# The last group of heads but one in the last segment: products with V in column tiles, brought back through DRAM

## The chip, the cores and the metric

The kernel runs on one core of a Trainium2 chip (the chip has eight). The metric is the time of one execution on the device in microseconds (us); the time of a kernel is the median over its runs. The engines of a core run side by side, each through its own instructions in order: TensorE (PE, matmuls; PEld is its loading of weights), VectorE (DVE), ScalarE (ACT), GpSimd (POOL) and SyncE (SP), which here only issues DMAs. Results of PE land in PSUM, everything else lies in SBUF or in DRAM.

## The reference

The input x (2048 tokens of 640) is normalized. One branch is an attention with a memory, over four segments of 512 tokens and 32 heads of 20 columns; the other is a gated unit; their product, after an output projection and a silu, is added to x:

```
for s in range(N):                       # N = 4 segments of L = 512
    logits = einsum('bhqd,bhkd->bhqk', qs, ks) * scale + mask
    p = softmax(logits, axis=-1)
    a_dot = einsum('bhqk,bhkd->bhqd', p, vs)
    a_mem = einsum('bhld,bhde->bhle', pq, M) / (einsum('bhld,bhd->bhl', pq, z) + 1e-6)
    o = g * a_mem + (1.0 - g) * a_dot
    M, z = M + pk^T vs, z + sum(pk)
...
h = sigmoid(xn @ w_gate) * (xn @ w_up)
return x + (o @ wo) * silu(h @ w_down)
```

The mask is causal within a segment, phi is applied to q and k for the memory.

## The kernel before, in words

Heads come in eight groups of four (20 columns each, so a group is 80 columns of the 640). A segment has 20 slots, five for a pair of groups; the whole kernel has 80 slots and an empty one behind them, number 80. In a slot PE computes scores for one unit of the lower triangle (`scores`, into `Sps`), ScalarE takes the exponential (`exps`, into `pt`, of which there are four), and GpSimd zeroes what lies above the diagonal. Four buffers of PSUM (tag "d") go round among all other products.

The products with V are made in one of two ways.

- In column tiles (`attend_T`, L556): V is the stationary operand, one head for each quarter of the array's columns, and `ApsT` comes out transposed, 16 matmuls for a group. Then VectorE turns it in blocks of 32 (`turn`, into `tb`), the quotients are taken (`quotients`: a reciprocal on VectorE and two multiplications, on GpSimd but for group 7, where they are on VectorE; into `ob`) and VectorE turns it back (`turn_back`, into `obT`). `dot_spill` (four DMAs on SP's queue, one for each head of a group) writes that to DRAM (`OTd`), where the columns lie in the order of the output projection; `out_load` reads it back as `oT`, five chunks of 128 columns, and `out_add` adds the memory's part (`oTm`), which came through DRAM by a transposing DMA.
- Naturally (`attend`, L593): `pt` is the stationary operand, V moves, 40 matmuls of 21 columns for a group into `Aps`; `finalize` (four VectorE operations: rd, rd, od, odot) divides and adds the result to the memory's part in `odot`, tokens on partitions.

All groups go the first way, but for groups 6 and 7 of the last segment, whose slots begin at `OLD` = 75. There `attend` runs behind slots 75 to 79. Their columns are 480 to 640, that is a quarter of chunk 3 (from `C3` = 384) and chunk 4 (from `C4` = 512). Chunk 3 comes back by a spill of `odot` and a transposing DMA (`tail_spill`, `tail_T`), to which `tail_sum` adds the 96 columns that came the first way; chunk 4 is transposed by PE (`tail_T4`, two transposes each for the first and the second half of the tokens, into `po`) and copied to `oT` by ScalarE.

Between the slots' own work a planner lays out the dense matmuls: `gp` and `up` (the gated unit), `yp` (its down projection, 12 matmuls each, followed by a tanh `t` on ScalarE and a product `aa` on VectorE), the projections, and events, each with a due time in slots from the table `TIMES` and a cost in ns. The dense work is spread evenly. In the slot ahead of each `attend_T` (a visit) the dense matmuls are issued in column tiles as well (`ORDER["columns"]`, in the profile "128*32", four for one). The last two down projections are held back: behind all slots come the first of them, `tail_T4(0, 2)`, and the output projection of the first 128 tokens (`tail_piece`, two products `sp` of five matmuls, each multiplied into `aa` by VectorE; `tail_add` adds x and issues the store), then the second of them, and the other pieces, with `tail_T4(2, 4)` among them.

The order on each engine is that of the program's text: nothing is reordered behind it.

Of the kernel before, what the change touches and what calls it, by code (L numbers as in the profile page):

```python
# [50 lines left out]
def segment_units(n):  # L51
# [3 lines left out]
    return units  # L55

TIMES = dict(
    turn=(0.03, 0.27, 1.29), turn_last=(0.0, 0.135, 0.43), attend=0.36, rest=350, dot6=0.43, load6=0.48,
    dot7=1.92, load7=1.95, add=(4.27, 4.52), out=(5.25, 5.95, 7.25, 8.35, 8.74, 9.06, 9.45, 11.05), update=-1.2,
    mem=(2.23, 4.32, 3.0, 6.98, 6.98, 2.45, 9.09, 10.79), mem_spill=11.56, mem_T=14.4, mem_T_last=12.63,  # L60
    k_tok=2.04, dot3=13.22, dot5=17.84, load5=18.1, add5=19.86, stats0=(0.53, 0.9, 1.65, 3.6),
    stats=(-0.55, 0.13, 1.32, 3.57), norm=(5.26, 5.72, 6.03, 6.29), norm_T=7.22, ready=12.0,
    K=(9.69, 10.07, 10.49, 13.82, 14.29), Q=(11.32, 11.72, 12.29, 12.45, 13.52), K_eng='vaava', Q_eng='avvav',
    V=(10.33, 13.33, 14.43, 14.63, 17.05, 17.66, 19.78, 20.06), V_eng='avaavvav', k_spill0=14.77, k_lay0=15.15,
# [5 lines left out]
def mm_ns(n):  # L70
    return n / 2.4 + 3.0
# [4 lines left out]
def kernel(  # L76
# [420 lines left out]
            out_store(n, j)  # L497

    C3, C4 = (DC - 2) * P, (DC - 1) * P
    CUT = 6 * 4 * DH - C3  # L500
    tail = {}

    def tail_spill():
        nc.sync.dma_start(Od[(NSEG - 1) % 2][:, C3:C4].rearrange("(j p) d -> p j d", p=P),
                          seg[NSEG - 1]["odot"][:, :, C3:C4])

    def tail_T():
        nc.sync.dma_start_transpose(out=seg[NSEG - 1]["oTm"][:, 3, :], in_=Od[(NSEG - 1) % 2][:, C3:C4])

    def tail_sum():  # L510
        oTm = seg[NSEG - 1]["oTm"][0:CUT, 3, :]
        nc.vector.tensor_tensor(oTm, oTm, seg[NSEG - 1]["oT"][0:CUT, 3, :], op=ALU.add)

    def tail_T4(j0, j1):
        po = ps_d.tile([P, 2, P], BF, name="po", tag="d")
        for j in range(j0, j1):
            nc.tensor.transpose(po[:, j - j0, :], seg[NSEG - 1]["odot"][:, j, C4:D], ident[:])
        nc.scalar.copy(seg[NSEG - 1]["oT"][:, DC - 1, j0 * P:j1 * P].rearrange("p (j t) -> p j t", t=P), po[:])

    def tail_piece(j, half):  # L520

        s, hs = seg[NSEG - 1], slice(half * HD, (half + 1) * HD)
        sp = ps_d.tile([P, HD], F32, name="sp", tag="d")
        for c in range(DC):
            oT = s["oTm" if c == 3 else "oT"]
            nc.tensor.matmul(sp[:], lhsT=oT[:, c, j * P:(j + 1) * P], rhs=Wo[:, c, hs],  # L526
                             start=(c == 0), stop=(c == DC - 1), skip_group_check=True)
        nc.vector.tensor_tensor(s["aa"][j][:, hs], s["aa"][j][:, hs], sp[:], op=ALU.mult)

# [26 lines left out]
    def attend_T(n, g, todo):  # L556


        s = seg[n]
        if g % 4 == 0:  # L560
            s["obT", g // 4] = opool.tile([P, 4, L], BF, name="obT", bufs=1)
        ps = ps_d.tile([P, L], F32, name="ApsT", tag="d")
        for i, ((_, kb, c0, ncol, q0), t) in enumerate(todo):
            for r in range(4):
                off = (kb * H + 4 * g + r) * E1
                nc.tensor.matmul(ps[32 * r:32 * r + 32, q0:L], lhsT=Vflat[n % 2][:, off:off + 32],  # L566
                                 rhs=t[:, r, c0:c0 + ncol], start=(i == 0), stop=(i == len(todo) - 1),
                                 tile_position=(0, 32 * r), skip_group_check=True)
        tb = opool.tile([P, L // 32, 32], F32, name="tb", tag="tb", bufs=1)
        rb = opool.tile([P, L // 32], F32, name="rb", bufs=2)  # L570
        ob = obs[g % 2]

        def turn():
            nc.vector.transpose(tb[:].rearrange("p h e -> p (h e)"), ps[:].rearrange("p (a t b) -> p a b t", t=32, b=2))  # L574

        def quotients():
            nc.vector.reciprocal(rb[:], tb[:, :, DH])
            to = ob[:].rearrange("p a e b -> p a b e")[:, :, :, 0:DH]
            of = tb[:].rearrange("p (a b) e -> p a b e", b=2)[:, :, :, 0:DH]
            by = rb[:].rearrange("p (a b) -> p a b", b=2).unsqueeze(3).to_broadcast([P, L // 64, 2, DH])  # L580
            eng = nc.vector if g == NG - 1 else nc.gpsimd
            eng.tensor_scalar(rb[:], rb[:], omgT[:, g:g + 1], None, op0=ALU.mult)
            eng.tensor_tensor(to, of, by, op=ALU.mult)  # L583

        def turn_back():
            nc.vector.transpose(s["obT", g // 4][:, g % 4, :].bitcast(F32),  # L586
                                ob[:].rearrange("p a e b -> p (a e b)").bitcast(F32))

        s["turn", g] = (turn, quotients, turn_back)

    acc = dict(group=None, todo=[])

    def attend(n, unit, pt):  # L593

        todo = acc["todo"] + [(p, pt) for p in unit]
        acc["todo"] = []
        for i, ((g, kb, c0, ncol, q0), t) in enumerate(todo):
            if acc["group"] is None:
                acc["group"], acc["blocks"], acc["fresh"] = g, 0, True
                acc["ps"] = ps_d.tile([P, 4, 4, E1], F32, name="Aps", tag="d")  # L600
            if acc["group"] != g or (acc["blocks"] == 0 and i > 0 and todo[i - 1][0][0] != g):
                acc["todo"] = todo[i:]
                break
            for r in range(4):
                for qb in range(kb, 4):
                    off = c0 + (qb - kb) * P
                    nc.tensor.matmul(acc["ps"][:, qb, r, :], lhsT=t[:, r, off:off + P],
                                     rhs=V[n % 2][:, kb, 4 * g + r, :],
                                     start=acc["fresh"], stop=True, skip_group_check=True)
                    acc["fresh"] = False  # L610
            acc["blocks"] += 1
            if acc["blocks"] == 4:
                finalize(n, g, 0, 4)
                acc["group"] = None
                acc["todo"] = todo[i + 1:]
                break

    def finalize(n, g, q0, q1):

        s, Aps = seg[n], acc["ps"]  # L620
        nq = q1 - q0
        rd = opool.tile([P, 4, 4], F32, name="rd", bufs=3)
        nc.vector.reciprocal(rd[:, 0:nq, :], Aps[:, q0:q1, :, DH])
        nc.vector.tensor_tensor(rd[:, 0:nq, :], rd[:, 0:nq, :],
                                omg[:, 4 * g:4 * g + 4].unsqueeze(1).to_broadcast([P, nq, 4]), op=ALU.mult)
        dst = s["odot"][:, q0:q1, 4 * g * DH:(4 * g + 4) * DH]
        od = opool.tile([P, 4, 4 * DH], BF, name="od", tag="tb", bufs=1)[:, 0:nq, :]
        nc.vector.tensor_tensor(od.rearrange("p q (r e) -> p q r e", e=DH), Aps[:, q0:q1, :, 0:DH],
                                rd[:, 0:nq, :].unsqueeze(3).to_broadcast([P, nq, 4, DH]), op=ALU.mult)
        nc.vector.tensor_tensor(dst, dst, od, op=ALU.add)  # L630
# [102 lines left out]
        finish(do_up(0, f))  # L733

    GLU_NS, V_NS, AV_NS = DC * mm_ns(L), DC * mm_ns(HD), 700
    MEM_NS, C_NS = 220, 2 * mm_ns(L) + 200
    dense = deque()
    downs, outs = [0] * NSEG, [0] * NSEG
# [22 lines left out]
    def at(t, ns, fn, *a):  # L761
        events.append((t, len(events), ns, lambda: fn(*a)))

    visits = {}
    for p in range(0, OLD, 5):
        n, g = units[p][0], units[p][1][0][0]
        visits[p + 4] = (n, g, (p, p + 1, p + 2))
        visits[p + 6] = (n, g + 1, (p + 3, p + 2, p + 4))

    def out_item(n, i):  # L770
        while downs[n] < 8:
# [6 lines left out]

    for slot, (n, g, _) in visits.items():
        for k in range(3):  # L780
            at(slot + TIMES["turn_last" if g == NG - 1 else "turn"][k], 0, turn, n, g, k)

    def old_attend(slot):
        attend(NSEG - 1, units[slot][1], pts[slot])

    for slot in range(OLD, SLOTS - 1):
        at(slot + 1 + TIMES["attend"], 500, old_attend, slot)

    st = {}

# [11 lines left out]
    for n in range(NSEG):  # L802
# [22 lines left out]
        if n == NSEG - 1:  # L825
            on("dot5", 0, dot_spill, (n, 4, 6))
            on("load5", 0, out_load, (n, 0, 6 * 4 * DH))
            on("add5", 0, out_add, (n, 0, 3))
            continue
        m = n + 1  # L830
        on("stats0" if n == 0 else "stats", 0, stats, *[(m, j) for j in range(4)])
# [23 lines left out]
                    at(t0 + t, 0, fn, *a)  # L855
        if n + 2 < NSEG:
            on("load_x", 0, load_x, (n + 2,))
    at(SLOTS - 2.001, 0, tail_spill)
    at(SLOTS - 1.001, 0, tail_T)
    at(SLOTS - 0.001, 0, tail_sum)  # L860

    events.sort(key=lambda e: e[:2])
    events = deque(events)
# [32 lines left out]
    for slot, (n, unit) in enumerate(units):  # L896
# [24 lines left out]
        if cur[0] is not None and cur[0][0] * cur[0][1] < TIMES["rest"]:  # L921
            complete()
    fill(1e12)
    finish(held[1][3])
    tail_T4(0, 2)
    tail_piece(0, 0)
    tail_piece(0, 1)
    tail_add(0, 0, 2, nc.gpsimd, nc.sync)
    finish(held[0][3])
    tail_piece(1, 0)  # L930
    tail_piece(1, 1)
    tail_add(1, 0, 1, nc.vector)
    tail_T4(2, 4)
    tail_piece(2, 0)
    tail_add(2, 0, 1, nc.gpsimd, nc.scalar)
    tail_add(1, 1, 2, nc.vector)
# [35 lines left out]
```

## Time and profile before

| | us |
|---|---|
| median of three runs | 318.75 (318.68, 318.75, 319.62) |
| the profiled execution, its own time | 319.31 |
| its span, first to last instruction | 317.6 |
| PE busy | 308.5 (97%) |
| ScalarE busy | 226.9 (71%) |
| VectorE busy | 223.7 (70%) |
| GpSimd busy | 133.7 (42%) |
| moved by DMA | 41.36 MB |

All times in the traces are from the start of the span, and the span is 1.7 us shorter than the execution's own time. A row of a timeline gives start, length, engine, line, operation, what it writes and reads, and how many were merged; in brackets the engine's idle time before it and what ended that. A row of the chain of waits gives start, length and what held the end up in that stretch. A row of windows gives the stretch, its length, the busy time of PE, PEld, DVE, ACT and POOL with their instructions, the granted clock of PE as a share, the DMA engines' busy share and GB/s. PE's granted clock is full (1.00) over the whole span.

### The profile page before, as it was taken

To read this page: it belongs to the slowest core of one execution; us is meant where nothing else is said; L and a number is where in the kernel's file an instruction comes from. 1 tells how busy PE (TensorE), PEld (TensorE's weight loads), DVE (VectorE), ACT (ScalarE), POOL (GpSimd) and SP (SyncE) were. 2 spreads that over 40 slices of the span, in tenths; PEclk is the share of its full clock that TensorE was granted. 3 is DMA by queue.
4 is the path that set the end of the run, shared out by engine and by line. 5 is a ranking of instruction groups with operands and counts; after the bars stand their busy time and mean duration, and the time that the engine had idled before them with its cause. 6 is when DMAs were issued, how large, how long until landed. Compare 5 with 4: busy or idle time off the path is not lost.

```text
span 317.6 us, 10039 instructions
## 1 busy us (share of the span) xinstructions
PE 308.5 (97%) x4212; PEld 166.7 (52%) x4241; DVE 223.7 (70%) x504; ACT 226.9 (71%) x228; POOL 133.7 (42%) x230
## 2 busy tenths in 40 slices
PE   7999999999999999999999999999999999999995
PEld 3544445665545445654665455545466655445673
DVE  6474445655868988888769989788777686634465
ACT  3723477778798776777987869678896776777711
POOL 1870035435253445335444354454544353535412
PEclk9999999999999999999999999999999999999999
DMA  7984886510742362405943475139524001250312
GB/s 254 370 320 142 284 229 169 137 33 2 219 138 76 102 160 106 105 23 157 254 143 109 121 138 147 49 114 216 168 82 122 19 23 44 92 137 4 99 20 83
DMA packets 56085, 41.36 MB, mean 130 GB/s; under 512 B 26952, under 2 KB 54664, under 8 KB 56040
## 3 DMA queue, kind: packets, MB, share of 16 engines
q1 hardware_dynamic: 53496, 35.97, 40.3%
q10 hardware_dynamic: 2544, 4.75, 4.0%
q8 instruction: 33, 0.54, 0.7%
q14 instruction: 12, 0.10, 0.1%
HBM read 19.90 MB, written 14.78 MB: 109 GB/s over the span
## 4 chain that ended last, share of the span: by engine, by line
PE 94%; issue 1%; DMA 1%; ACT 1%; DVE 1%; SPq 0%; ACTq 0%
PE yp L124 11%; PE up L124 11%; PE gp L124 10%; PE psq L124 10%; PE Sps L542 9%; PE gp L128 6%; PE up L128 6%; PE yp L128 5%; PE ApsT L566 5%; PE psv L124 5%; PE psq L128 4%; PE sp L124 3%; PE sp L128 3%; PE psv L128 2%; PE sp L526 1%
## 5 line engine op out<-in xcount | busy, mean ns | idle before, releaser
L550 ACT ACTIVATE pt<-Sps 128x2048 bf16<-128x2048 f32 x80 | 150.3, 1879 | 41.5 <-PE Sps L542 39.8
L552 POOL TENSOR_SCALAR_AFFINE_SELECT pt<-pt 128x512 bf16<-128x512 bf16 x128 | 82.9, 663 | 157.2 <-ACT pt L550 154.7
L432 DVE SCALAR_TENSOR_TENSOR hT<-tg,up 128x512 bf16<-128x512 bf16 x48 | 32.6, 679 | 24.0 <-PE up L124 10.0
L124 PE MATMUL up<-xnT,Wu 128*128 128x512 bf16 x146 | 40.3, 380 | 1.4 <-issue 1.1
L124 PE MATMUL yp<-Wd,hT 128*128 128x320 bf16 x263 | 40.9, 299 | 0.5 <-issue 0.5
L124 PE MATMUL gp<-xnT,Wg 128*128 128x512 bf16 x146 | 38.9, 379 | 0.6 <-issue 0.5
L421 ACT ACTIVATE tg<-gp 128x512 bf16<-128x512 f32 x48 | 28.6, 595 | 14.4 <-PE gp L124 9.6
L542 PE MATMUL Sps<-QT,KT 23*128 23x384 bf16 (+3 forms) x512 | 32.4, 301 | 0.1
L124 PEld LDWEIGHTS <-hT 128*128 128x128 bf16 x263 | 24.2, 98 | 12.6 <-issue 3.9
L449 DVE SCALAR_TENSOR_TENSOR aa<-t,yp 128x320 bf16<-128x320 bf16 x32 | 15.3, 479 | 16.5 <-ACT t L448 16.4
L128 PE MATMUL gp<-xnT,Wg 128*32 128x512 bf16 x352 | 24.4, 380 | 0.0
L574 DVE STREAM_TRANSPOSE tb<-ApsT 128x512 f32<-128x512 f32 x30 | 21.3, 711 | 3.5 <-PE ApsT L566 3.4
L124 PEld LDWEIGHTS <-Wu 128*128 128x128 bf16 x159 | 14.1, 98 | 17.2 <-issue 4.0
L566 PE MATMUL ApsT<-pt,V 128*32 128x512 bf16 (+2 forms) x480 | 22.7, 299 | 0.0
L124 PEld LDWEIGHTS <-Wg 128*128 128x128 bf16 x152 | 14.1, 98 | 15.8 <-issue 1.9
L542 PEld LDWEIGHTS <-KT 23*128 23x128 bf16 x512 | 9.7, 92 | 23.8 <-issue 23.7
L128 PE MATMUL up<-xnT,Wu 128*32 128x512 bf16 x324 | 21.7, 380 | 0.0
L448 ACT ACTIVATE t<-yp 128x320 bf16<-128x320 f32 x32 | 13.9, 436 | 10.1 <-PE yp L124 8.5
L583 POOL TENSOR_TENSOR ob<-tb,rb 128x320 bf16<-128x320 f32 x27 | 19.9, 736 | 2.2
L586 DVE STREAM_TRANSPOSE obT<-ob 128x256 f32<-128x256 f32 x30 | 13.0, 434 | 11.1 <-POOL ob L583 11.0
L124 PE MATMUL psq<-xnT,Wq 128*128 128x512 bf16 x82 | 19.4, 379 | 0.2
L128 PE MATMUL yp<-Wd,hT 128*32 128x320 bf16 x484 | 19.4, 300 | 0.0
(123 smaller groups left out, 448.0 us busy)
## 6 DMA issues: line engine op xcount, KB each, us to landing
KT<-Kd SPq DMA_DIRECT2D x32, 80.0 KB
QT<-Qd SPq DMA_DIRECT2D x32, 80.0 KB
out_dram<-xt SPq DMA_DIRECT2D x14, 160.0 KB
Wg<-in_B_w_gate_dram ACTq DMA_DIRECT2D x1, 1920.0 KB
Wu<-in_B_w_up_dram ACTq DMA_DIRECT2D x1, 1920.0 KB
xt<-in_A_x_dram SPq DMA_DIRECT2D x3, 640.0 KB
Wd<-in_B_w_down_dram SPq DMA_DIRECT2D x1, 1920.0 KB
Xd<-xn SPq DMA_DIRECT2D x12, 160.0 KB
```

Of the source, the lines that this page charges most:

```text
L124: nc.tensor.matmul(out_, lhsT=lhsT, rhs=rhs, start=start, stop=stop, skip_group_check=True)
L128: nc.tensor.matmul(out_[cols], lhsT=lhsT[:, cols], rhs=rhs, start=start, stop=stop, tile_position=(0, 32 * r), skip_group_check=True)
L421: nc.scalar.activation(tg[:], gp[:], ACT.Tanh, scale=0.5)
L432: nc.vector.scalar_tensor_tensor(out=h[:], in0=seg[n]["tg"][:], scalar=1.0, in1=up[:], op0=ALU.add, op1=ALU.mult)
L448: nc.scalar.activation(t2[:], yp[:], ACT.Tanh, scale=0.25)
L449: nc.vector.scalar_tensor_tensor(out=s["aa"][j][:, hs], in0=t2[:], scalar=1.0, in1=yp[:], op0=ALU.add, op1=ALU.mult)
L542: nc.tensor.matmul(Sps[:, r, c0:c0 + ncol], lhsT=KT[32 * r:32 * r + DH + 3, g, kb * P:(kb + 1) * P], rhs=QT[32 * r:32 * r + DH + 3, g, q0: ...
L550: nc.scalar.activation(pt[:, :, 0:ntot], Sps[:, :, 0:ntot], ACT.Exp, scale=SCALE)
L552: nc.gpsimd.affine_select(out=pt[:, :, c0:c0 + P], in_=pt[:, :, c0:c0 + P], compare_op=ALU.is_ge, fill=0.0, base=0, pattern=[[0, 4], [1, P ...
L566: nc.tensor.matmul(ps[32 * r:32 * r + 32, q0:L], lhsT=Vflat[n % 2][:, off:off + 32], rhs=t[:, r, c0:c0 + ncol], start=(i == 0), stop=(i == ...
L574: nc.vector.transpose(tb[:].rearrange("p h e -> p (h e)"), ps[:].rearrange("p (a t b) -> p a b t", t=32, b=2))
L583: eng.tensor_tensor(to, of, by, op=ALU.mult)
```

## The change

Group 6 of the last segment goes through `attend_T` at slot 79 (a visit like those of the other groups, with the times of a group 7 and its quotients on VectorE); only group 7 is natural, in two parts, 24 matmuls behind the scores of slot 79 and 16 in the empty slot 80. Group 6's part comes back by four spills and two loads (`tail_load`): 32 columns into chunk 3 of `oT`, which `out_add` then completes as it does the others, and 48 into a new tile `o6`, which is cleared once at the start. The transposing DMA of chunk 3, its spill and its sum are gone. `tail_T4` copies the upper half of a transposed chunk 4 on ScalarE and adds the lower half and `o6` on VectorE, and its transposes now stand behind 9 of the 12 matmuls of each held down projection. `RESERVE` books a third of 800 ns in each of three slots in the planner's account, where it issues nothing.

```diff
+R5, R6 = 6 * 4 * DH, 7 * 4 * DH
+HALF = P // 2
+o6 = cpool.tile([HALF, L], BF, name="o6")
+nc.gpsimd.memset(o6[:].bitcast(mybir.dt.uint32), 0)
+def tail_load():
+    src = OTd[(NSEG - 1) % 2]
+    nc.sync.dma_start(seg[NSEG - 1]["oT"][R5 - C3:P, 3, :], src[R5:C4, :])
+    nc.sync.dma_start(o6[0:R6 - C4, :], src[C4:R6, :])
 def tail_T4(j0, j1):
     po = ps_d.tile([P, 2, P], BF, name="po", tag="d")
     for j in range(j0, j1):
         nc.tensor.transpose(po[:, j - j0, :], seg[NSEG - 1]["odot"][:, j, C4:D], ident[:])
-    nc.scalar.copy(seg[NSEG - 1]["oT"][:, DC - 1, j0 * P:j1 * P].rearrange("p (j t) -> p j t", t=P), po[:])
+    t = slice(j0 * P, j1 * P)
+    oT = seg[NSEG - 1]["oT"][:, DC - 1, t]
+    pf = po[:].rearrange("p j t -> p (j t)")
+    nc.scalar.copy(oT[HALF:P, :], pf[HALF:P, :])
+    nc.vector.tensor_tensor(oT[0:HALF, :], pf[0:HALF, :], o6[:, t], op=ALU.add)
...
-            eng = nc.vector if g == NG - 1 else nc.gpsimd
+            eng = nc.vector if g == NG - 1 or (n, g) == (NSEG - 1, NG - 2) else nc.gpsimd
...
+    visits[OLD + 4] = (NSEG - 1, NG - 2, (OLD, OLD + 1, OLD + 2))
...
-    for slot in range(OLD, SLOTS - 1):
-        at(slot + 1 + TIMES["attend"], 500, old_attend, slot)
+    for slot in range(OLD + 1, OLD + 4):
+        at(slot + TIMES["attend"], RESERVE, lambda: None)
+    at(OLD + 4 + TIMES["last"][0], 500, last_attend, (OLD + 2, OLD + 3))
+    at(OLD + 5 + TIMES["last"][1], 500, last_attend, (OLD + 4,))
...
+            on("dot6_last", 0, dot_spill, (n, 6, 7))
+            on("load6_last", 0, tail_load, ())
+            on("add6_last", 0, out_add, (n, 3, 4))
...
-    at(SLOTS - 2.001, 0, tail_spill)
-    at(SLOTS - 1.001, 0, tail_T)
-    at(SLOTS - 0.001, 0, tail_sum)
...
+    for _ in range(9):
+        next(held[1][3])
+    tail_T4(0, 2)
     finish(held[1][3])
-    tail_T4(0, 2)
     tail_piece(0, 0)
     tail_piece(0, 1)
     tail_add(0, 0, 2, nc.gpsimd, nc.sync)
+    for _ in range(9):
+        next(held[0][3])
+    tail_T4(2, 4)
     finish(held[0][3])
     tail_piece(1, 0)
     tail_piece(1, 1)
     tail_add(1, 0, 1, nc.vector)
-    tail_T4(2, 4)
```

More of the change, by code (lines that the diff above doesn't have):

```diff
@@ L57 @@
 TIMES = dict(
-    turn=(0.03, 0.27, 1.29), turn_last=(0.0, 0.135, 0.43), attend=0.36, rest=350, dot6=0.43, load6=0.48,
+    turn=(0.03, 0.27, 1.29), turn_last=(0.0, 0.135, 0.43), attend=0.36, last=(0.36, 0.75), rest=350, dot6=0.43, load6=0.48,
     dot7=1.92, load7=1.95, add=(4.27, 4.52), out=(5.25, 5.95, 7.25, 8.35, 8.74, 9.06, 9.45, 11.05), update=-1.2,
     mem=(2.23, 4.32, 3.0, 6.98, 6.98, 2.45, 9.09, 10.79), mem_spill=11.56, mem_T=14.4, mem_T_last=12.63,
-    k_tok=2.04, dot3=13.22, dot5=17.84, load5=18.1, add5=19.86, stats0=(0.53, 0.9, 1.65, 3.6),
+    k_tok=2.04, dot3=13.22, dot5=17.84, load5=18.1, add5=19.86, dot6_last=19.55, load6_last=19.6, add6_last=20.9, stats0=(0.53, 0.9, 1.65, 3.6),
     stats=(-0.55, 0.13, 1.32, 3.57), norm=(5.26, 5.72, 6.03, 6.29), norm_T=7.22, ready=12.0,
@@ L499 @@
     C3, C4 = (DC - 2) * P, (DC - 1) * P
[L500 to L512, printed above, removed]
+    R5, R6 = 6 * 4 * DH, 7 * 4 * DH
[6 more added lines that the diff above has]
+        nc.sync.dma_start(o6[0:R6 - C4, :], src[C4:R6, :])
     def tail_T4(j0, j1):
@@ L524, in tail_piece @@
         for c in range(DC):
-            oT = s["oTm" if c == 3 else "oT"]
-            nc.tensor.matmul(sp[:], lhsT=oT[:, c, j * P:(j + 1) * P], rhs=Wo[:, c, hs],
+            nc.tensor.matmul(sp[:], lhsT=s["oT"][:, c, j * P:(j + 1) * P], rhs=Wo[:, c, hs],
                              start=(c == 0), stop=(c == DC - 1), skip_group_check=True)
@@ L589, in attend_T, with attend @@
         s["turn", g] = (turn, quotients, turn_back)
[L591 to L603, printed above, removed]
+    acc = {}
+    def attend(n, todo):
+        if not acc:
+            acc["ps"] = ps_d.tile([P, 4, 4, E1], F32, name="Aps", tag="d")
+            acc["blocks"] = 0
+        for (g, kb, c0, ncol, q0), t in todo:
             for r in range(4):
@@ L608, in attend @@
                                      rhs=V[n % 2][:, kb, 4 * g + r, :],
-                                     start=acc["fresh"], stop=True, skip_group_check=True)
-                    acc["fresh"] = False
+                                     start=(acc["blocks"] == 0 and r == 0 and qb == kb), stop=True,
+                                     skip_group_check=True)
             acc["blocks"] += 1
[L612 to L616, printed above, removed]
+        if acc["blocks"] == 4:
+            finalize(n, NG - 1, 0, 4)
     def finalize(n, g, q0, q1):
@@ L735 @@
     GLU_NS, V_NS, AV_NS = DC * mm_ns(L), DC * mm_ns(HD), 700
+    RESERVE = 800 / 3
     MEM_NS, C_NS = 220, 2 * mm_ns(L) + 200
@@ L780, with last_attend @@
         for k in range(3):
-            at(slot + TIMES["turn_last" if g == NG - 1 else "turn"][k], 0, turn, n, g, k)
-    def old_attend(slot):
-        attend(NSEG - 1, units[slot][1], pts[slot])
-    for slot in range(OLD, SLOTS - 1):
-        at(slot + 1 + TIMES["attend"], 500, old_attend, slot)
+            late = g == NG - 1 or slot == OLD + 4
+            at(slot + TIMES["turn_last" if late else "turn"][k], 0, turn, n, g, k)
+    def last_attend(slots):
+        todo = [(p, pts[u]) for u in slots for p in units[u][1] if p[0] == NG - 1]
+        attend(NSEG - 1, todo)
+    for slot in range(OLD + 1, OLD + 4):
+        at(slot + TIMES["attend"], RESERVE, lambda: None)
+    at(OLD + 4 + TIMES["last"][0], 500, last_attend, (OLD + 2, OLD + 3))
+    at(OLD + 5 + TIMES["last"][1], 500, last_attend, (OLD + 4,))
     st = {}
```

## The prediction

> **What bounds the kernel now.** I read the page first, for the span and for the engine that carries it.
>
> ```profile
> span 317.6 us, 10039 instructions
> PE 308.5 (97%) x4212; PEld 166.7 (52%) x4241; DVE 223.7 (70%) x504; ACT 226.9 (71%) x228; POOL 133.7 (42%) x230
> PE 94%; issue 1%; DMA 1%; ACT 1%; DVE 1%; SPq 0%; ACTq 0%
> ```
>
> PE is busy for 97% of the span and is 94% of the chain that ended last. So a change pays by what it takes out of PE's stream, and costs by any gap that it puts in. The instruction orders of the two kernels, both built and neither timed, are the same on PE up to the end of group 5's column-tiled product of the last segment; all that differs lies behind it. So I read the chain of waits from there to the end (start, length, what; lengths are from one start to the next, so they add).
>
> ```profile
> 290.36 0.40 PE Aps L607 x16
> ...
> 292.19 1.06 PE yp L124 x7
> 293.25 0.39 PE Aps L607 x16
> 293.64 1.51 PE yp L124 x11
> ...
> 296.53 0.19 PE Aps L607 x8
> ...
> 298.23 0.34 PE Sps L542 x8
> ...
> 302.68 0.39 PE Aps L607 x16
> 303.06 3.15 PE yp L124 x23
> ...
> 306.24 0.14 ACT t L448
> ...
> 306.57 0.38 ACT oT L518
> ...
> 306.99 0.99 PE sp L526 x6
> 307.98 1.63 PE yp L124 x12
> 309.61 1.36 PE sp L526 x10
> 310.97 0.11 PE po L517 x2
> 311.08 2.15 PE sp L526 x15
> 313.25 0.50 DVE aa L528
> ...
> 314.63 0.33 DVE xt L534
> ```
>
> To see here: PE has no gap until 306.22, where the transposes of the last 128 columns of `odot` (po) have been issued and PE waits for ScalarE, which still has a tanh (t) in front of the copy out of PSUM. From 313.25 on the chain belongs to VectorE.
>
> **The change part by part.**
>
> *Products.* The 40 matmuls of group 6 go: the first 16, the second 16 and the 8 of the rows, 0.40 + 0.39 + 0.19 = 0.98 us, all of it on the path. In their place stand 16 column-tiled matmuls, priced by the same product two groups earlier:
>
> ```profile
> 239.05 0.54 PE ApsT L566 x16
> ```
>
> 0.54 us. Net: −0.44. PE must also change between row tiles (Sps), column tiles and the whole array. A change shows as the 0.10 by which 7 yp behind Sps (1.06) exceed 7/11 of 1.51. The number of changes stays: the dense matmuls of the slot ahead of the new product are issued in column tiles too, as the planner does ahead of every such product. The Trainium skill (TensorEngine Tiling (Array Packing), Key Properties) says that a change of tiling mode drains TensorE. That would speak against a column-tiled product set among whole-array ones: two more changes, 0.2 us, and the gain of this part would be 0.24. With the slot ahead in columns it gives 0.44, as the rows do.
>
> *The copy at the end.* Both transposes move to a place three yp matmuls before the end of the last two down projections. What that takes away: from 306.22, two po (0.11) and ten sp (1.36) would end at 307.69, the chain has 307.98, so the first gap is 0.29. Fifteen sp at 1.36/10 are 2.04, the chain has 2.15: the second gap is 0.11. Together −0.40. ScalarE's copy will now stand ahead of the tanh, covered by three yp (0.41) and four sp (0.55). If that cover were gone, the 0.40 would come back.
>
> *The new wait.* Half of the last chunk (columns 512 to 560) and a quarter of chunk 3 (480 to 512) now come back through DRAM: VectorE turns group 6, four spills go out on SP, two loads follow, a VectorE add finishes chunk 3, and another adds the loaded `o6` to the transposed half. The natural way's transposed DMA of chunk 3 goes, with its spill and its 0.41 us add; these lay beside PE and give nothing. To place the loads I shift the rows above. Ahead of the second Sps of the tail PE has −0.98 + 0.54 + five more yp (at 3.15/23 each, 0.69) = +0.25, so ApsT ends at 298.23 + 0.25 = 298.48. VectorE's way from there is that of a group 7, which also has its quotients on VectorE:
>
> ```profile
> 239.64 0.72 DVE L574 STREAM_TRANSPOSE tb<-ApsT 128x512 f32<-128x512 f32 x1 [0.27 <-PE ApsT L566]
> 240.95 0.52 DVE L583 TENSOR_TENSOR ob<-tb,rb 128x320 bf16<-128x320 f32 x1
> 242.70 0.44 DVE L586 STREAM_TRANSPOSE obT<-ob 128x256 f32<-128x256 f32 x1
> 243.16 1.40 SPq L467 DMA_DIRECT2D OTd<-obT  x4
> 246.28 0.35 SPq L474 DMA_DIRECT2D oT<-OTd  x1
> 294.54 1.42 SPq L467 DMA_DIRECT2D OTd<-obT  x4
> 297.34 0.39 SPq L474 DMA_DIRECT2D oT<-OTd  x1
> 178.65 1.50 SPq L467 DMA_DIRECT2D OTd<-obT  x4
> 182.77 0.35 SPq L474 DMA_DIRECT2D oT<-OTd  x1
> ```
>
> From ApsT's end at 239.05 + 0.54 = 239.59 to the end of ob at 241.47 are 1.88, and the turn back is 0.44 more: obT is there at 298.48 + 2.32 + 0.05 = 300.85. From the first of four spills to the load behind them the rows show 2.80 (294.54 to 297.34), 3.12 and 4.12. I take 2.80: the two others were each issued right behind a load of the whole of oT but its last chunk, and here SP's last loads were issued three microseconds earlier. The second load, that of `o6`, goes out at about 303.7, or 303.9 if the first one's 0.39 is in its way. How long a load takes to land (DMA issues with KB each, two windows, one wait):
>
> ```profile
> oT<-OTd SPq DMA_DIRECT2D x3, 512.0 KB
> ...
> oT<-OTd SPq DMA_DIRECT2D x1, 384.0 KB
> ```
>
> ```profile
> 247.00:247.50 0.50, 0.50 (x22) 0.38 (x18) 0.21 (x1) 0.50 (x1) 0.00 (x0) 1.00 0.17 57
> 247.50:248.00 0.50, 0.50 (x24) 0.41 (x16) 0.00 (x0) 0.50 (x2) 0.05 (x1) 1.00 0.59 205
> ```
>
> ```profile
> 300.64 1.23 POOL L552 TENSOR_SCALAR_AFFINE_SELECT pt<-pt 128x512 bf16<-128x512 bf16 x2 [2.48 <-DMA oT<-OTd]
> ```
>
> The load issued at 246.28 moves its bytes between 247.0 and 248.0 (the last two columns of a window are DMA share and GB/s). That is 1.7; I add 0.5 until its waiter can see it (an estimate). The other bound is 3.3: the 384 KB issued at 297.34 are put down as landed at 300.64. So `o6` lands at 306.1 at best guess, chunk 3's quarter 0.5 earlier.
>
> VectorE runs in order, and its queue is: finalize of group 7, add of chunk 3 (waits for the first load), aa of a down projection, add of the half (waits for `o6`), aa of the held down projection, then the products with sp. So a late load holds all of these.
>
> ```profile
> 303.45 0.25 DVE L623 RECIPROCAL rd<-Aps 128x16 f32<-128x16 f32 x1
> ...
> 304.47 0.32 DVE L630 TENSOR_TENSOR odot<-odot,od 128x320 bf16<-128x320 bf16 x1
> 305.48 0.41 DVE L512 TENSOR_TENSOR oTm<-oTm,oT 96x512 bf16<-96x512 bf16 x1
> 305.08 0.49 DVE L449 SCALAR_TENSOR_TENSOR aa<-t,yp 128x320 bf16<-128x320 bf16 x1 [0.28 <-ACT t L448]
> ```
>
> PE by then: 40 yp in place of 48 lie between the second Sps and the transposes, so these start at 306.22 + 0.25 − 1.10 = 305.37, after finalize: Aps ends at 303.07 + 0.25 + two more yp (0.27) = 303.6, and from the first to the last of finalize's rows are 1.34, so 305.0 (before, an aa stood ahead of it and it started 0.38 late; with that, 305.3). PE then has po, three yp and four sp and wants chunk 3 at 306.30 and the half of chunk 4 at 306.44. VectorE: chunk 3 from 305.6 to 306.0 (0.41), aa 0.40, the half from 306.2 at the earliest to 306.6 (0.41, the nearest row being the 96x512 add). A wait of 0.15 is left. Its ends: 0 (the 2.80 and a landing in 1.7), and 2.3 (spills 4.12, landing 3.3: `o6` at 308.3, the half done at 308.7). I take 0.15, as the rows nearest in place and load are the short ones. In the second half the add waits for ScalarE's copy (0.38) alone; copy and add fit into the three yp and four sp (0.96) that PE does meanwhile: nothing.
>
> *Beside the path.* POOL clears `o6` (64x256) ahead of its first wait:
>
> ```profile
> 7.93 0.25 POOL L238 TENSOR_SCALAR rs<-mv 128x1 f32<-128x1 f32 x1 [5.87 <-DVE mv L648]
> ```
>
> It stands idle there for 5.87 us, so nothing; without that cover its clearing would hold up the second half of the first normalization. Of group 6 the four VectorE operations of finalize (304.47 + 0.32 − 303.45, 1.3 us in all) make place for the five of the column way (2.3). They run beside PE and cost nothing as long as PE doesn't wait for a PSUM buffer: shifting the rows as above, each of the four buffers has its last reader done some half a microsecond before PE wants it.
>
> *The end.* Behind the last yp VectorE sets the time: before, the last add started 314.63 − 309.61 = 5.02 behind it. The second po (0.11) and the second gap (0.11) are gone from that stretch, so 4.80; both are in the sums above.
>
> **Sum:** −0.44 − 0.40 + 0.15 = −0.69. Span 316.9; the profiled execution took 319.31 for its span of 317.6, so 318.6 in its own terms. It lies 0.56 above the median of the three runs, 318.75, from which the same difference gives 318.06.
>
> **The rivals.**
> - *The wait eats the gain.* The round trip takes 3.12 and its load 0.5 longer than I put it (both spills and loads follow others on SP). For: the same four 20 KB spills took 3.12 the one time nearest in the trace. Against: the bytes ahead of them. `o6` then lands at 306.9, the add ends at 307.3, the wait is 0.85: 318.77. The Trainium skill (DMA: Bandwidth & Descriptors, Latency and other measured facts) says that an HBM access takes 0.2 us on average and 2 us under high load; the 4.12 behind a load and the 2.80 without one agree in direction. By it the short round trip would hold here, as the queue is quiet.
> - *Slower: SP's round trip becomes the path.* One mechanism: VectorE's add of the half waits for `o6` while the sp products stand behind it. It costs 1 for 1 from a landing at 306.0 on; at 306.9 the kernel is where it was, from 307.8 it is slower by more than 0.3%. At the far bounds (4.12 and 3.3) the wait is 2.3: −0.84 + 2.3 = +1.5, 320.2. For: two transfers in a row, whose lengths are the least certain numbers here. Against: all short rows are quiet ones, as this place is.
> - *More than forecast.* No wait at all (`o6` at 305.9), and VectorE's end comes free of its backlog: 313.25 to 314.63 are 1.38 for two pieces where PE needs 0.68 for the second; with the last add bound by PE, 0.2 more goes. −0.84 − 0.2 = −1.0: 317.7. Against: its order of work is as before.
>
> **How the numbers follow.** Chances: forecast 0.57, the wait eats the gain 0.18, slower 0.11, more than forecast 0.14. About 0.3%, or 0.96 us, is what a measurement of this kernel can tell from no change; its three runs span 0.94. Forecast and first rival lie inside, the last one just outside. Of the forecast's chance I give 0.11 to faster for sizes and for the runs' spread: faster 0.24, the same 0.65, slower 0.11. The range goes from 317.3, the largest gain with 0.4 of spread, to 319.6, which takes in a wait of 1.7 and leaves out only the far bound.
>
> **What would show it.** In the changed profile's chain: 16 ApsT of 0.54 in place of 40 Aps, no ScalarE piece near 306, PE's sp without a gap behind the first po but for about 0.15 put down to VectorE's add; obT of group 6 near 300.9, the load of `o6` issued near 303.9, the last VectorE add near 313.95. The forecast is wrong if PE's chain shows a DMA or VectorE wait of over 0.5 us before its first sp of chunk 4, if switches appear around ApsT, or if the stretch before 290 moves.

## The result, and the profile after

The changed kernel takes 318.34 us (median of 22 runs), the kernel before 318.97 (22 runs beside it). The ratio is 0.9975, its 95% interval 0.9963 to 0.9987: 0.80 us faster, between 0.41 and 1.18. One of the changed kernel's 22 took 797.38 us; the ratio is taken without it. The difference is inside the 0.3% that the prediction called the same, and on the side that it forecast (−0.69; 318.1).

The profiled execution took 317.75 us, its span is 316.0, and the page's first lines and the chain by engine correspond to those shown before.

```profile
span 316.0 us, 10105 instructions
PE 307.7 (97%) x4239; PEld 166.5 (53%) x4268; DVE 225.1 (71%) x507; ACT 226.6 (72%) x228; POOL 133.4 (42%) x231
PE 95%; DMA 2%; issue 1%; ACT 1%; DVE 1%; SPq 0%; ACTq 0%
```

The spans differ by 1.6 us, twice what the times differ. Comparing the start of each slot's exponential on ScalarE, the two profiles run within 0.05 us of each other up to 166.6 us; then that of before loses 0.65 us within one slot, and at slot 76 it is 0.68 behind. The loss belongs to that execution, not to the kernel (the last section), so the change is read from slot 76's exponential on, which starts at 289.74 before and at 289.06 after:

```profile
289.74 1.88 ACT L550 ACTIVATE pt<-Sps 128x2048 bf16<-128x2048 f32 x1 [1.67 <-PE Sps L542]
```

```profile
289.06 1.88 ACT L549 ACTIVATE pt<-Sps 128x2048 bf16<-128x2048 f32 x1 [1.67 <-PE Sps L541]
```

From there to the start of the last VectorE add are 314.63 − 289.74 = 24.89 us before. The chain of waits of the changed kernel (start, length, what):

```profile
297.24 0.54 PE ApsT L565 x16
...
298.91 0.59 PE Aps L601 x24
...
302.50 0.39 PE Aps L601 x16
302.89 1.78 PE yp L124 x13
304.67 0.11 PE po L513 x2
304.78 0.41 PE yp L124 x3
305.19 1.36 PE sp L525 x10
306.55 1.22 PE yp L124 x9
307.77 0.11 PE po L513 x2
307.88 0.41 PE yp L124 x3
308.29 3.41 PE sp L525 x25
...
313.10 0.32 DVE xt L533
```

That is 313.10 − 289.06 = 24.04: 0.85 less. To see here: the 16 ApsT take 0.54, of the 80 Aps 24 and 16 are left, no ScalarE piece stands near 306, and ten sp behind the first po take 1.36, that is, PE doesn't wait for the round trip at all. The new path beside it (start, length, engine, what, idle time before):

```profile
300.18 1.41 SPq L467 DMA_DIRECT2D OTd<-obT  x4
...
301.94 0.49 SPq L507 DMA_DIRECT2D oT<-OTd  x1
...
303.43 0.31 SPq L508 DMA_DIRECT2D o<-OTd  x1
...
304.20 0.42 DVE L481 TENSOR_TENSOR oT<-oT,oTm 128x512 bf16<-128x512 bf16 x1
...
305.22 0.28 DVE L518 TENSOR_TENSOR oT<-po,o 64x256 bf16<-64x256 bf16 x1 [0.20 <-ACT oT L517]
...
305.55 0.66 PEld L525 LDWEIGHTS <-oT 128*128 128x128 bf16 x6 [0.16 <-DVE oT L518]
```

The add of the half waits for ScalarE's copy, not for the load, and ends at 305.50; PE wants it four sp behind 305.19, at 305.74. So at most 0.24 us were to spare in this execution, and less for the weights of that sp: their load had already waited 0.16 for the add.

### The profile page after: what moved, and what is told of

It is laid out like the page before. It is cut to its first block, busy times and chain, and to the rows that moved or that the text cites. A ratio compares the mean times of both kernels' runs of the same rounds, so it can differ in the third digit from the quotient of the medians.

```text
span 316.0 us, 10105 instructions
## 1 busy us (share of the span) xinstructions
PE 307.7 (97%) x4239; PEld 166.5 (53%) x4268; DVE 225.1 (71%) x507; ACT 226.6 (72%) x228; POOL 133.4 (42%) x231
## 4 chain that ended last, share of the span: by engine, by line
PE 95%; DMA 2%; issue 1%; ACT 1%; DVE 1%; SPq 0%; ACTq 0%
PE up L124 11%; PE gp L124 10%; PE yp L124 10%; PE psq L124 10%; PE Sps L541 9%; PE gp L128 6%; PE yp L128 6%; PE up L128 6%; PE ApsT L565 5%; PE psv L124 5%; PE psq L128 4%; PE sp L124 3%; PE sp L128 3%; PE psv L128 2%; DMA Wv<-in_A_wv_dram 2%; PE sp L525 2%
## 5 line engine op out<-in xcount | busy, mean ns | idle before, releaser
L124 PE MATMUL yp<-Wd,hT 128*128 128x320 bf16 x246 | 38.3, 300 | 0.0
L124 PEld LDWEIGHTS <-hT 128*128 128x128 bf16 x246 | 22.7, 98 | 11.3 <-issue 3.0
L573 DVE STREAM_TRANSPOSE tb<-ApsT 128x512 f32<-128x512 f32 x31 | 22.0, 711 | 4.2 <-PE ApsT L565 4.1
L565 PE MATMUL ApsT<-pt,V 128*32 128x512 bf16 (+2 forms) x496 | 23.4, 299 | 0.0
L128 PE MATMUL yp<-Wd,hT 128*32 128x320 bf16 x552 | 21.9, 300 | 0.0
L565 PEld LDWEIGHTS <-V 128*32 128x32 bf16 x496 | 14.4, 97 | 8.1 <-ACT tg L421 0.2
```

Of the source, the lines that this page charges most:

```text
L124: nc.tensor.matmul(out_, lhsT=lhsT, rhs=rhs, start=start, stop=stop, skip_group_check=True)
L128: nc.tensor.matmul(out_[cols], lhsT=lhsT[:, cols], rhs=rhs, start=start, stop=stop, tile_position=(0, 32 * r), skip_group_check=True)
```

## The experiments

Times are compared with runs of the kernel before on the same chip; the stretch from slot 76's exponential to the last VectorE add comes from each kernel's one profile and is free of losses ahead of it.

| kernel | stretch, us | ratio to before (95%) |
|---|---|---|
| before | 24.89 | |
| changed | 24.04 | 0.9975 (0.9963 to 0.9987) |
| turn_only | 24.66 | 0.9985 (0.9965 to 1.0006) |
| turn_late | 25.33 | 1.0011 (0.9996 to 1.0026) |
| changed_again | 25.02 | 1.0004 (0.9981 to 1.0028) |
| pool_add | 23.86 | 0.9975 (0.9959 to 0.9991) |
| slot78_whole | 24.15 | one run, no ratio |
| load_twice | 25.55 | one run, no ratio |
| spill_twice | 25.45 | one run, no ratio |
| fetch_moved | 24.04 | 1.0085 (1.0058 to 1.0112) |
| pieces_last | 24.11 | 0.9960 (0.9942 to 0.9978) |
| pieces_last_load_twice | 24.10 | one run, no ratio |

**turn_only: the kernel before, with only the transposes moved.**

```diff
-    finish(held[1][3])
-    tail_T4(0, 2)
+    for _ in range(9):
+        next(held[1][3])
+    tail_T4(0, 2)
+    finish(held[1][3])
```

and likewise for `held[0]`, whose `tail_T4(2, 4)` moves up from behind `tail_add(1, 0, 1)`.

> The kernel before, with nothing changed but the place of the two pairs of transposes of chunk 4: three yp matmuls ahead of the end of each held down projection. Theory (the gain is two parts that add: -0.44 of the products, -0.40 of the copy that no longer holds PE): PE has no gap at either copy, the stretch from the last two gp matmuls to the start of the last VectorE add is 24.86 - 0.40 = 24.46 us, the time 0.4 us below before. Rival (the copy was no cost, the whole gain lies in the products): 24.86, no difference.

24.66 us: −0.23 in place of −0.40. The second gap went, and the first became another. The rows of VectorE and PE in its timeline:

```profile
306.71 0.42 DVE L512 TENSOR_TENSOR oTm<-oTm,oT 96x512 bf16<-96x512 bf16 x1 [0.68 <-DMA oTm<-Od]
...
307.19 0.10 PEld L526 LDWEIGHTS <-oTm 128*128 128x128 bf16 x1 [0.34 <-DVE oTm L512]
```

With the copy out of the way, chunk 3's transposing DMA is late next: `tail_sum` waits 0.68 us for it, and ten sp take 1.54 (306.77 to 308.31) in place of 1.36. So the two parts don't simply add in the kernel before. The 0.40 were had in full with the products' new way back, whose first load had landed in time in the changed kernel's first profile.

**turn_late: the changed kernel, with the transposes back where they stood.** The diff is the reverse of the one above.

> The changed kernel with the two pairs of transposes put back where they stood before. Theory: PE waits behind the transposes for ScalarE's copy (0.29 and 0.11 us as before) and now for VectorE's add behind it (0.28 each): the stretch goes from 24.01 to 25.0 us, so the kernel is no better than before (24.86). Rival (the products carry the gain): it stays within 0.2 us of 24.01.

25.33 us, 0.44 worse than before and 1.29 worse than the changed kernel. In its chain PE waits behind the first po for the tanh, the copy and VectorE's add, one after the other:

```profile
305.29 0.14 ACT t L448
...
305.75 0.38 ACT oT L517
...
306.17 0.29 DVE oT L518
...
306.50 0.99 PE sp L525 x6
```

Behind the second po VectorE's add comes after two aa products and an addition of x, and PE goes on at 311.49 (0.35 idle). By the stretch the rival falls: without its cover the lower half's add on VectorE makes the end slower than before, although the products are cheaper. The times can't tell this kernel from before (1.0011).

**changed_again: the changed kernel, a second time.**

> The changed kernel once more, beside the three others. Every theory: 0.3 to 1.2 us faster than before; the stretch from the last two gp matmuls to the start of the last VectorE add is 24.0 us. If the 0.7 us by which its first profile was ahead of before in the middle of the kernel were its own, it would be there again; if it was a pause in that one execution of before, the two kernels stand within 0.1 us of each other up to the last two gp.

Up to 166.6 us it stands within 0.03 of the first profile, then it loses 0.72, in the slot in which before lost 0.65: nothing that belongs to the one kernel or the other. Its stretch is not 24.0 but 25.02, though: the size of the prediction's first rival, in the same program. In the times, too, the gain is not there again: none of these 12 runs lies below 318.17 us, where 10 of the first 22 lie below 318.1. Its queue and its chain of waits:

```profile
294.59 2.70 SPq L467 DMA_DIRECT2D OTd<-obT  x4
298.68 0.39 SPq L474 DMA_DIRECT2D oT<-OTd  x1
...
300.90 2.66 SPq L467 DMA_DIRECT2D OTd<-obT  x4
304.50 0.31 SPq L507 DMA_DIRECT2D oT<-OTd  x1
304.91 0.36 SPq L508 DMA_DIRECT2D o<-OTd  x1
```

```profile
301.23 3.20 DMA OTd<-obT
...
304.50 1.68 DMA oT<-OTd
...
306.20 0.43 DVE oT L481
...
306.94 0.29 DVE oT L518
...
307.27 0.99 PE sp L525 x6
```

From the first spill to the first load are 3.60 us, where the first profile has 1.76. The chain puts 3.20 of them down to the landing of a spill. The fourth spill's issue held SP for 1.58 us in place of 0.33, but SP was free again at 303.56, and the load went out at 304.50 only. The delay began with group 5, which goes this way in the kernel before too: its four spills took 2.70 us to issue (the third alone 1.62), the load of `oT` went out 4.09 us behind the first of them, where the kernel before has 2.80, and VectorE's add shows that it had not landed before about 302.0, when group 6's spills were on their way:

```profile
302.01 0.96 DVE L481 TENSOR_TENSOR oT<-oT,oTm 128x1536 bf16<-128x1536 bf16 x1 [0.31 <-DMA oT<-OTd]
```

In the first 1.2 us behind group 6's first spill the DMA engines moved 254 GB/s here, 38 in the first profile. That these bytes made the spills late is argued; no run tried it. VectorE waited for chunk 3's load, not for that of `o6`; PE stood 0.36 us before its fourth sp and 0.28 before its fifth, and the gain of this execution is gone (24.89 against 25.02).

**load_twice and spill_twice: the round trip made longer.**

```diff
-        nc.sync.dma_start(o6[0:R6 - C4, :], src[C4:R6, :])
+        for _ in range(2):
+            nc.sync.dma_start(o6[0:R6 - C4, :], src[C4:R6, :])
```

> The changed kernel with the load of o6 issued twice; the second waits for the first to land. In the changed kernel's profile the load goes out at 303.43 and PE wants the half of chunk 4 at 305.74 without waiting. From the start of slot 76's exponential to the start of the last VectorE add are 24.04 us there. Theory (the round trip has little slack, and past it costs 1 for 1): a landing of 1.6 us more puts VectorE's add at 306.8, PE waits 1.3 us before its fifth sp, 25.3 us. Rival (the round trip is hidden well): no wait, 24.0 us.

```profile
303.26 1.67 DMA o<-OTd
...
304.95 1.75 DMA o<-OTd
```

The chain shows each load from its issue to what it released: 1.67 and 1.75 us. With the second, VectorE's add starts at 306.79, PE's fifth sp at 307.13, and the stretch is 25.55. Slot 76 starts 0.06 later here, so the add starts 1.51 us later than in the changed kernel, and the stretch is 1.51 longer. The wait costs 1 for 1, and of the 0.24 nothing is left: once PE has stood, its next six sp take 0.99 us in place of 6 × 0.136 = 0.82. The rival falls. The Trainium skill (DMA: Bandwidth & Descriptors, Anatomy of one DMA — SWDGE (gpsimd) path) gives 2.0 us and a part for the bytes, fitted to DMAs that GpSimd issues; for these 48 KB that would be 2.1 (an estimate from that page). The trace has 1.67 and 1.75 on SP's queue.

```diff
             on("dot6_last", 0, dot_spill, (n, 6, 7))
+            on("dot6_last", 0, dot_spill, (n, 6, 7))
```

> The changed kernel with the four spills of group 6 issued twice; the second four wait for the first to land, so both loads come one spill later. Theory: the loads go out 2.4 to 3.2 us later, VectorE stands at the add of chunk 3 and everything behind it with it, PE waits 2 to 2.8 us in front of its fourth sp: 26 to 26.8 us in place of 24.04. Rival (VectorE's order doesn't matter): under 25.

25.45 us: the mechanism is right (PE stands 0.53 us before its fourth sp and 0.54 before its fifth), the size was less, since the second spills wait only for their own first ones. The load of `o6` went out at 304.94, 1.4 us later than in the changed kernel (slot 76 starts 0.07 later here).

**slot78_whole: the slot ahead of the new product on the whole array.**

```diff
-        ORDER["columns"] = slot + 1 in visits
+        ORDER["columns"] = slot + 1 in visits and slot != OLD + 3
```

> The changed kernel with the 17 yp matmuls of slot 78 on the whole array in place of column tiles, so that PE goes from whole array to columns for the 16 ApsT: one change of tiling more. Theory: one change costs 0.10 us, 24.14 us. Rival (the drain is hidden, the tiles' choice ahead of a product is free): 24.04.

24.15 us, 0.11 more, and the chain shows where: 16 ApsT take longer.

```profile
294.89 2.42 PE yp L124 x17
297.30 0.66 PE ApsT L565 x16
```

One change of tiling costs 0.11 to 0.12 us here (0.66 against 0.54), as the prediction took it from the rows of yp behind Sps (0.10). The Trainium skill (TensorEngine Tiling (Array Packing), Key Properties) has the drain, and the trace agrees; it gives no price.

**pool_add: the last addition but one on GpSimd.**

```diff
-    tail_add(3, 0, 1, nc.vector, nc.sync)
+    tail_add(3, 0, 1, nc.gpsimd, nc.scalar)
```

> The changed kernel with the last addition of x but one on GpSimd and its store on ScalarE's queue. Theory (the end behind PE is bound by VectorE): VectorE takes the last product 0.27 us earlier and the kernel is 0.1 to 0.25 us faster than the changed one. Rival: GpSimd's addition (0.79 us, behind two others) ends last and the end is 0 to 0.2 us later.

The last VectorE add starts 0.18 earlier, but takes 0.49 in place of 0.32: it ends 24.35 behind slot 76's exponential, against 24.36. VectorE's backlog is gone (its last product waits 0.19 us for PE's sp, where in the changed kernel it comes straight behind an addition), and still nothing is gained, because the addition behind that product takes 0.17 longer. In these two profiles the VectorE additions at the end that start while one of GpSimd's runs take 0.43 and 0.49 us, the others 0.32; that the one slows the other is argued, not tried. The ratio is that of the changed kernel's first measurement; changed_again, measured beside pool_add, has 1.0004, and the intervals overlap. So the third rival's condition came about here, and its 0.2 us did not.

**fetch_moved: the blocks of instructions elsewhere.**

```diff
     keep_warm(9)
+    for _ in range(48):
+        nc.tensor.matmul(wps[0:32, 0:8], lhsT=warm[:, 0:32], rhs=warm[:, 0:8], start=True, stop=True)
```

> The changed kernel with 48 small matmuls (32x8, results unused) behind the warm-up, while PE waits for x: 96 PE instructions more ahead of everything, so that PE's blocks of instructions end 96 earlier in the work. In the changed kernel's profile a packet of 16384 bytes of the instruction queue runs from 300.4 to 301.4, among the spills of 300.2 to 301.6, and one part of each spill lands about 1 us behind the rest. Theory (that packet holds up the spills' parts on its DMA engine): with the packet at about 298 the load of o6 goes out 0.6 to 1.0 us earlier, 2.3 to 2.7 us behind the first spill in place of 3.25; the stretch stays 24.0 (the wait was hidden already), and in runs in which the round trip is late the time is better. Rival (the late part is of the spills' own): 3.25 again.

```profile
302.88 1.41 SPq L467 DMA_DIRECT2D OTd<-obT  x4
304.65 0.31 SPq L507 DMA_DIRECT2D oT<-OTd  x1
305.34 0.31 SPq L508 DMA_DIRECT2D o<-OTd  x1
```

The load of `o6` goes out 2.46 behind the first spill, not 3.25, as expected; the stretch is 24.04. But not for the packet that I named. In slot78_whole, too, no packet of queue 8 ran among the spills, and there the load went out at 303.54, 3.19 behind the first spill. What the two do not share is the other instruction queue. The queues' packets from the first spill to the load of `o6`, in the changed kernel, slot78_whole and fetch_moved:

```profile
q1 hardware_dynamic: 168, 0.11, 13.8%
q8 instruction: 1, 0.02, 1.8%
q14 instruction: 1, 0.01, 1.2%
```

```profile
q1 hardware_dynamic: 164, 0.11, 14.0%
q14 instruction: 1, 0.01, 1.1%
```

```profile
q1 hardware_dynamic: 145, 0.11, 14.7%
```

With a packet of queue 14 the load goes out late, without it early. The five other profiles in which four spills went out in 1.41 us agree: each has such a packet there, and the load goes out 3.02 to 3.19 behind the first spill. No run moved that packet alone, and changed_again, the latest, has one packet of each queue there like the first profile, so this isn't the whole of it. Nor had each spill a late part, as I had put it: the first load, which needs the first two spills alone, goes out 1.76 behind the first spill in the changed kernel and 1.77 in fetch_moved. The kernel itself became 0.85% slower than before: it is 0.57 us behind from the first slot on, and at 191 us, where a packet of queue 8 now runs beside the spills of the next segment's normalized input, VectorE waits for one of those spills:

```profile
192.91 0.61 DVE L243 TENSOR_SCALAR xn<-xt,mv,rs 128x640 bf16<-128x640 bf16 x1 [1.46 <-DMA Xd<-xn]
```

The changed kernel has no such wait there. Another 1.7 us are lost at that place; that the packet costs them isn't shown.

**pieces_last: more room for the round trip.**

```diff
-    for _ in range(9):
-        next(held[1][3])
-    tail_T4(0, 2)
     finish(held[1][3])
-    tail_piece(0, 0)
-    tail_piece(0, 1)
-    tail_add(0, 0, 2, nc.gpsimd, nc.sync)
     for _ in range(9):
         next(held[0][3])
+    tail_T4(0, 2)
     tail_T4(2, 4)
     finish(held[0][3])
+    tail_piece(0, 0)
+    tail_piece(0, 1)
+    tail_add(0, 0, 2, nc.gpsimd, nc.sync)
```

> The changed kernel with both held down projections ahead of all pieces of the output projection, the two pairs of transposes still three yp matmuls ahead of the second one's end: PE's work is the same, but it wants the half of chunk 4 about 1.75 us later (nine yp, the second pair of transposes and three yp more in between). Theory (the round trip's landing is what spoils the gain in some executions): with an early landing the stretch from slot 76's exponential to the last VectorE add stays 24.0 to 24.2 us (VectorE's last part gets denser), with a late one it no longer grows. Rival (the later start of the pieces piles up VectorE's work at the end): 24.4 or more, and the kernel is slower than the changed one.

> The same with the load of o6 issued twice, which in the changed kernel's order cost PE a wait and gave 25.55 us. Theory: the landing at about 306.8 is now ahead of PE's need (about 307.5), no wait, 24.0 to 24.2 us. Rival (the end is bound by VectorE behind the add, wherever PE wants it): 25 or more.

24.11 us, and with the load issued twice 24.10: the landing 1.75 us later costs nothing now, where it cost 1.5 in the changed kernel's order. The chain of pieces_last_load_twice has no gap behind the transposes:

```profile
302.92 3.41 PE yp L124 x25
306.33 0.22 PE po L514 x4
306.55 0.41 PE yp L124 x3
306.96 4.77 PE sp L526 x35
```

35 sp take 4.77, 0.136 each. The kernel takes 318.05 us (11 runs) against 319.36 of before (16 runs), ratio 0.9960 (0.9942 to 0.9978): the lowest median here, and clear of the kernel before. Its interval overlaps that of the changed kernel, so that it is faster than this one isn't shown; the lengthened load shows that it has the room that this one lacks.

## Why the prediction was right

- *Products, −0.44.* Right: 0.98 out, 0.54 in, row for row in the chain after. That the change of tiling costs nothing more because slot 78 is in columns was confirmed by slot78_whole (+0.11 without it).
- *The copy, −0.40.* Right in the changed kernel, both gaps are gone. Right also that the cover carries it: without it turn_late is 1.29 us slower in the stretch, more than the 0.40 that I put, because VectorE's add and the aa ahead of it in its order stand behind the copy. What I hadn't seen is that in the kernel before this part alone would have given 0.23, with the transposing DMA of chunk 3 late next.
- *The new wait, +0.15.* The mis-sized term: 0.00 in the first profile, 0.98 in the second (25.02 − 24.04). For the first profile three sizes were off. Two were too long: the add of the half takes 0.28, not 0.41; the load 1.67 from issue to release, not 2.2, of which the 0.5 behind the bytes had no row. One was too short: the load's issue, put at 2.85 to 3.05 behind the first spill, came at 3.25. That the wait costs 1 for 1 past a small slack was right (load_twice: the add 1.51 later, the stretch 1.51 longer), and its cause, VectorE in order in front of the sp products, is what the chain of changed_again shows.
- *Sum.* −0.69 forecast; −0.85 in the first profile, +0.13 in the second; −0.80 (0.41 to 1.18) in the first times, no difference in the second (1.0004, 0.9981 to 1.0028). The two terms on PE are shown; that the whole came out so near to the first times is luck in part, as it hangs on how many executions have the wait.
- *Rivals.* That the wait eats the gain was put at 318.77; of the changed kernel's two profiles one shows it (25.02, with 24.89 before). By the sign that I had named (a wait of over 0.5 before the first sp of chunk 4; here 0.36 and 0.28) this profile speaks against the forecast, too. Its path was another than I gave: chunk 3's load was late, not that of `o6`, behind a spill that took 3.20 us to land. The condition that I gave (loads and spills ahead on the queue) is met there, since the last load was issued 1.78 us ahead of the first spill, not 3.06 as in the first profile, where I had counted on three; whether it is the cause is open, and so is what held SP's issues for 1.6 us. The slower rival (a wait of 2.3) was seen in neither profile of the changed kernel. More than forecast was not seen: pool_add took VectorE's next-to-last add away and gained nothing.

## What to carry to other kernels

When a stall goes, ask what is late next at that place: in the kernel before, the DMA behind the copy that was seen in the chain took 0.18 of the 0.40 back, and replacing both gave the whole gain. A round trip through DRAM that fits with less than 0.24 us to spare may not fit in every execution: in five profiles with the order of the changed kernel and its round trip as it stands it came late once. Such slack costs little to widen where work that doesn't depend on it can be moved ahead (24.04 and 25.55 without, 24.11 and 24.10 with it). Take a second profile of the same program before a size is believed. Compare two profiles from the last common event on, not by their spans: here the spans differ by 1.6 us, the stretches from there on by 0.85.

## What the runs showed of the hardware

Some executions lose time in one and the same slot, between 166 and 170 us, whichever kernel: 0.65 (before), 1.16 (turn_only), 0.72 (changed_again) and 0.33 us (fetch_moved), and nothing in the eight other profiles. In before, 0.53 of it is idle time of PE that is put down to issue, that is, to nothing the profile shows:

```profile
167.91 0.57 PE L124 MATMUL yp<-Wd,hT 128*128 128x320 bf16 x3 [0.53 <-issue]
```

In the three others that is 0.22 us, 0.26 and nothing; there the four Sps behind it take longer, 1.26, 0.78 and 0.81 in their chains against 0.47 in the changed kernel's. In turn_only a loading of weights among them waits for a DMA:

```profile
169.95 0.09 PEld L542 LDWEIGHTS <-KT 23*128 23x128 bf16 x1 [0.27 <-DMA QT<-Bd]
```

SP began to issue the DMAs of this kind at 167.20 there, at 164.41 in the changed kernel; ahead of them the issue of one other DMA took 1.99 us, in changed_again 1.81, in the changed kernel 0.40. Issues of SP that take 1.6 us instead of 0.3 stand at the end of changed_again as well. What makes them was not tried.

Fetching instructions is DMA traffic too: the page of the kernel before lists 33 packets of instructions on queue 8 and 12 on queue 14. Where a packet of queue 14 falls among this kernel's small spills, the load behind them goes out later (3.02 to 3.25 us behind the first spill in seven profiles, against 2.46 without it). 96 idle PE instructions at the start moved the packets, and the kernel became 0.85% slower than before. That the packets cause the delay, rather than stand beside it, is argued from these places; it is not shown.
